# Squared-ReLU attention and a low-rank mixer on one core: block turns held between a cast and its turn, and casts of loads put in another order and at other times

## The chip, the cores and the metric

The kernel runs on one core of a Trainium2 chip. The metric is the device time of one execution in microseconds (us). The time before is the median of three executions, 986.9 us (986.28 to 986.96).

A core has five engines that run their own instruction queues in order: PE (TensorE, matrix products), DVE (VectorE), ACT (ScalarE), POOL (GpSimd) and SP (SyncE), which in this kernel issues every transfer. Tiles in SBUF have 128 partitions; PE writes its sums into PSUM.

## The reference

```python
B, S, D, dqk, R, H = 8, 3136, 256, 64, 32, 1024
# attention unit
scores = (1 / S) * z @ z.transpose(0, 2, 1)          # S x S for each batch, symmetric
attn   = maximum(scores, 0) ** 2
x      = u * (attn @ v)                              # B x S x D
# mixer
h   = x.transpose(0, 2, 1) @ U @ V                   # rank 32 over the sequence
x2  = x + h.transpose(0, 2, 1)
out = x2 + maximum(x2 @ w_ch1, 0) @ w_ch2
```

The inputs and the output are float32. The products are made in bfloat16 and summed in float32.

## The kernel before

**Tiles and items.** The 3136 rows of a batch are 24 tiles of 128 and a tail of 64. Four tiles are a group, so a batch has six groups of 512 rows and a small one of 64 (`NQ` = 6, `NG` = 7). An item is a pair (batch b, group g); the kernel goes through the 56 items in slots, t = 7 b + g. Slot 6 is thus the small item of batch 0, and slot 7 the first of batch 1. A slot of a full group takes some 13 to 19 us, a small one some 2 us for batch 0.

**What one slot does.** For its own item it forms attn @ v (`av_stream`, `av_end`) in a stream of units of one pair of 64-row matmuls each, and multiplies by u (`av_out`, L734). Between the units it places the scores of a later item (`score_burst`; eviction with ReLU L386 or L382, square L362), and the mixer of items seven and more slots back: `t1_all` (L782, the product with U for a whole batch), `u2_unit` (product with V, then x + h on DVE, L855), `ch1_part` (product with w_ch1) and `ch2_stream` (product with w_ch2). The small items have their own routines (`av_small`, L701, whose four partial sums go through ACT L720 and DVE L722, L724; `score_small`; `ch2_small`).

**Blocks and block turns.** A block holds 512 x 512 of attn in bfloat16. There are 20 of them in a list of free blocks. As scores are symmetric, a block (J, g) with J > g is computed once and transposed into a second block for item J by a DMA of SP, the block turn (`issue_turn`, L416; a block on the diagonal has a smaller one, L408). The turn takes its destination from the list of free blocks, and waits until PE has read what stood in it. A block whose score is squared puts its turn on the list `ready_turns`.

**The turn of x + h.** `ch1_part` needs x + h transposed (`u2T`). `u2_unit` adds x and h on DVE; three units before that ends, by the planner's books, `down` gives out the cast of x + h to bfloat16 on ACT or DVE, and two units after the cast's end `turned` gives out the transposing DMA (`x_turn`, L770), again on SP. For group 0 of a batch the cast is on DVE at once, and (b, g) is put on the list `urgent` right there; `turned` clears that list.

**The planner.** The order of the instructions on each queue is worked out while the program is written. `clock` counts in units of one pair of 256-column matmuls; `free_at` books when ACT, DVE and SP are free; `hold(due, f)` keeps a piece of work until the clock has come to its due time; `run_held` gives out what is due, and then block turns, as long as SP's books are free and `urgent` is empty. `cast` takes ACT or DVE, whichever the books have free first (L202, L204). When the matmuls of a block are written out and its turn is still in `ready_turns`, `av_stream` gives it out at once. When a piece of v that they need has no cast yet, it runs the held work until there is one.

**Loads and their casts.** Loads for batch 1 and the weights are given out in slots 0 to 5, each 22 units after the one before it: in slots 1 and 2 two quarters of V each (L1197) and a piece of v, in slot 3 U and two pieces of v, in slots 4 and 5 two pieces of w_ch1 (L1171) or w_ch2 (L1174) and a piece of v (`load_v_piece`, L254). Their casts are collected in `casts_next` and held in the next slot: 45 units after its start (15 units from slot 8 on, 90 units in a small slot), and 12 units more for each further one. `load_part` makes the steps for z and v, `first_loads` those for V, U and the weights.

Of the kernel before, what the change touches and what calls it, by code (L numbers as in the profile page):

```python
# [18 lines left out]
def kernel(  # L19
# [13 lines left out]
    B, S, D = u.shape  # L33
# [21 lines left out]
    NG = len(groups)  # L55
    items = [(b, g) for b in range(B) for g in range(NG)]

    def tiles_of(g):
        g0, gw = groups[g]
        return [(q, g0 // P + q, min(P, gw - q * P)) for q in range((gw + P - 1) // P)]  # L60
# [16 lines left out]
    NQ = NF // GT  # L77
# [18 lines left out]
    clock = [0.0]  # L96
# [4 lines left out]
    urgent = []  # L101
# [9 lines left out]
    def book(eng, ready, cost):  # L111
        free_at[eng] = max(free_at[eng], ready) + cost
        return free_at[eng]
# [5 lines left out]
    def hold(due, f):  # L119
        held.append((due, len(held), f))  # L120
# [25 lines left out]
    def take_ps():  # L146
        k = min(range(NPS), key=lambda i: ps_free[i])
        assert ps_free[k] < float("inf")
        clock[0] = max(clock[0], ps_free[k])
        ps_free[k] = float("inf")  # L150
        for bank in range(2):
            wrote.pop((k, bank), None)
        return k, ps_pool.tile([P, 2, GW], FP32, name=f"ps{k}")
# [23 lines left out]
    def pair(k, ops, n):  # L177

        if any(wrote.get((k, bank), (h,))[0] != h for h, bank, _ in ops):
            post(k)  # L180
        for h, bank, args in ops:
            ins = nc.tensor.matmul(**args)  # L182
            last = wrote.get((k, bank))
            if last and last[0] != h:
                behind(ins, last[2])
            wrote[k, bank] = [h, ins, None]
        pe(n / 256)
# [11 lines left out]
    def cast(out, in_, n):  # L199

        if free_at["act"] <= free_at["dve"]:
            nc.scalar.copy(out=out, in_=in_)  # L202
            return book("act", clock[0], n / 110)
        nc.vector.tensor_copy(out=out, in_=in_)  # L204
        return book("dve", clock[0], n / 130)

    def stage():
        return pool.tile([P, GT * D], FP32, name="stage", bufs=3)
# [13 lines left out]
    def load_z_piece(b, t0, n, raw, tail=True):  # L222
        m = min(n, NF - t0)
        nc.sync.dma_start(
            out=raw[:, : m * dqk].rearrange("p (t d) -> p t d", d=dqk), in_=rows_of(z[b])[:, t0 : t0 + m, :]
        )
        queued(m * dqk / 2)
        if n > m and tail:

            def tails():  # L230
                load_tail(raw, m * dqk, z[b], dqk)
                load_tail(raw, n * dqk, v[b], D)

            if b > 1:
                hold(clock[0] + 75, tails)
            else:
                tails()

    def z_copy(b, t0, n, raw, c, copy):
        copy(out=z_bfs[b][:, t0 : t0 + n, c, :], in_=raw[:, : n * dqk].rearrange("p (t d) -> p t d", d=dqk))  # L240

    def z_tiles(b):
        z_bfs[b] = pool.tile([P, NT, 2, dqk], BF16, name="z_bf", bufs=1)
        zzTs[b] = pool.tile([P, NT, P], BF16, name="zzT")
        v_bfs[b] = pool.tile([P, NT, D], BF16, name="v_bf")

    def v_tail(b, n, raw, copy):
        copy(out=v_bfs[b][:, NF, :], in_=raw[:, n * dqk : n * dqk + D])
        v_cast.add((b, NQ))
# [3 lines left out]
    def load_v_piece(b, k, raw):  # L253
        nc.sync.dma_start(  # L254
            out=raw.rearrange("p (t d) -> p t d", d=D), in_=rows_of(v[b])[:, k * GT : (k + 1) * GT, :]
        )
        queued(GT * D / 2)

    def v_copy(b, k, raw, copy):
        copy(out=v_bfs[b][:, k * GT : (k + 1) * GT, :], in_=raw.rearrange("p (t d) -> p t d", d=D))  # L260
        v_cast.add((b, k))

    def by_cast(n):
        return lambda out, in_: cast(out, in_, n)
# [6 lines left out]
    def load_part(b, g):  # L271
        later = {1: [0], 2: [1], 3: [2, 3], 4: [4], 5: [5]}

        def z_step(t0, n):
            raw = stage()
            load_z_piece(b, t0, n, raw)

            todo = []
            where = spare_next if b == 1 else todo
            copy = nc.gpsimd.tensor_copy if b == 1 else None  # L280
            for c in range(2):
                where.append(
                    lambda t0=t0, n=n, raw=raw, c=c: z_copy(b, t0, n, raw, c, copy or by_cast(n * dqk))
                )
            if n != 4 * GT:
                where.append(lambda n=n, raw=raw: v_tail(b, n, raw, copy or by_cast(D)))
            return todo

        def v_step(k):
            raw = stage()  # L290
            load_v_piece(b, k, raw)
            return [lambda k=k, raw=raw: v_copy(b, k, raw, by_cast(GT * D))]

        steps = []
        if g == 0:
            z_tiles(b)
            steps += [lambda: z_step(0, 4 * GT), lambda: z_step(4 * GT, NT - 4 * GT)]
        for k in {1: [0], 2: [1], 3: [2], 4: [3, 4], 5: [5]}.get(g, []) if b > 1 else later.get(g, []):
            steps.append(lambda k=k: v_step(k))
        return steps  # L300
# [322 lines left out]
    def crossed(way, a, make):  # L623

        ops = []
        for h in range(2):
            bank = h if way == 0 else 1 - h
            ops.append((h, bank, make(slice(h * hp, (h + 1) * hp), a + 2 * bank)))
        return ops
# [178 lines left out]
    def u2_unit(b, g, turn=True):  # L808
        ts = tiles_of(g)
        n, t0, rows = len(ts), ts[0][1], ts[0][2]  # L810
        k, ps = take_ps()
        if n == GT:
            for a in range(2):
                pair(
                    k,
                    crossed(
                        0,
                        a,
                        lambda h, q: dict(
                            out=four(ps)[:, q, :],  # L820
                            lhsT=V4_bf[h, (t0 + q) * P : (t0 + q + 1) * P],
                            rhs=t1s[b][h, :],
                            start=(a == 0),
                            stop=(a == 1),
                        ),
                    ),
                    D,
                )
        else:
            pair(  # L830
                k,
                [
                    (
                        0,
                        0,
                        dict(
                            out=ps[:, 0, :D],
                            lhsT=V4_bf[:hp, t0 * P : (t0 + 1) * P],
                            rhs=t1s[b][:hp, :],
                            start=True,  # L840
                            stop=True,
                        ),
                    )
                ],
                D,
            )
        x = xs[b, g][:rows, :n, :]
        if b == B - 1:
            entry, raw = stage_block()
            o_blocks[b, g] = entry  # L850
            o = raw.rearrange("p (q d) -> p q d", d=D)
        else:
            o = pool.tile([P, GT, D], FP32, name="out_sb", bufs=3)
        done = ps_free[k] = book("dve", clock[0] + 3, 11.2 * n / GT)
        nc.vector.tensor_tensor(out=o[:rows, :n, :], in0=four(ps)[:rows, :n, :], in1=x, op=ALU.add)  # L855
        u2s[b, g] = o
        if not turn:
            return

        def turned():  # L860
            u2Ts[b, g] = u2T_tile()
            x_turn(b, g, u2Ts[b, g])
            urgent.clear()

        def down():
            hold(cast(x, o[:rows, :n, :], n * D) + 2, turned)

        if g == 0:
            urgent.append((b, g))
            nc.vector.tensor_copy(out=x, in_=o[:rows, :n, :])  # L870
            hold(book("dve", done, 6.3) - 6, turned)
        else:
            hold(done - 3, down)
# [316 lines left out]
    def load_V(i0):  # L1190
# [25 lines left out]
    first_loads = {  # L1216
        1: lambda: load_V(0),
        2: lambda: load_V(2),
        3: lambda: [load_U],
        4: lambda: load_w(0),  # L1220
        5: lambda: load_w(1),
    }
# [84 lines left out]
    for b in range(B):  # L1307
        for g in range(NQ):
            t = b * NG + g - 1
# [24 lines left out]
    for t in range(n_items):  # L1334
# [6 lines left out]
        g_now = t % NG  # L1341
        b_next = t // NG + 1
# [6 lines left out]
            xTs[direct] = take_block()[1][:, : GT // 2, :].rearrange("p a (q d c) -> p (a q) d c", d=ND, c=P)  # L1349
            x_turn(*direct, xTs[direct])  # L1350
        for i, f in enumerate(casts_next):
            hold(clock[0] + (90 if g_now == NQ else 15 if t > NG else 45) + 12 * i, f)
        casts_next = []
        spare += spare_next
        spare_next.clear()
        steps = first_loads[t]() if t in first_loads else []
        if b_next < B:
            steps += load_part(b_next, g_now)

        def load(step):  # L1360
            casts_next.extend(step())
# [155 lines left out]
```

## Time and profile before

| what | us |
|---|---|
| median of three executions | 986.9 |
| the profiled execution, its own time | 988.19 |
| its span, first to last instruction | 986.4 |
| PE busy in the span | 974.8 |
| DVE / ACT busy | 627.8 / 483.6 |
| slot 6 and most of slot 7, 95.0 to 105.0: PE, DVE, ACT busy of 10.0 | 10.0, 8.66, 7.84 |
| 105.0 to 115.0: PE, DVE, ACT busy of 10.0 | 8.23, 6.56, 5.86 |
| one batch in the middle (441.6 to 561.4): PE, DVE, ACT busy of 119.8 | 119.8, 77.5, 56.2 |

The view of waits adds up, for an engine and a line, the idle time that ended when another engine or a DMA released it. The chain of waits goes back from the last instruction, at each step to what released it. The timeline lists instructions in order with their start and length; SPq rows are DMAs being issued on SP, and they include the time for which the issue waits in the queue. "u2T<-x_bf" is the turn of x + h, "blk<-blk" a block turn.

The transfers, with the median time from issue to landing:

```profile
stage<-in_v_dram SPq DMA_DIRECT2D x42, 512.0 KB, 6.2
blk<-blk SPq DMA_TRANSPOSE x156, 5.1
blk<-in_moe_w_ch_dram SPq DMA_DIRECT2D x4, 512.0 KB, 4.7
u2T<-x_bf SPq DMA_TRANSPOSE x47, 4.0
```

### The profile page before, as it was taken

The page shows a single profiled execution, that of the slowest core. Times are in us where ns is not written, and L with a number is a line of the kernel's source. Part 1 is how long each engine was busy: PE and PEld are TensorE (multiplying, and loading weights), DVE is VectorE, ACT ScalarE, POOL GpSimd, SP SyncE. Part 2 cuts the span into 40 slices and gives each one's busy share as a digit, 9 for nine tenths or more (in the row PEclk, how much of TensorE's full clock was granted, in tenths as well). Part 3 has the DMA queues.
Part 4 walks back from the last instruction along what each step waited for, and adds up shares of the span by engine and source line. Part 5 has one row for each costly group of instructions (what it writes and reads, how often), then busy time and mean ns, then how long its engine had stood idle before and what let it go on. Part 6 is the DMA issues. An engine that isn't in the chain of part 4 may idle for free.

```text
span 986.4 us, 35362 instructions
## 1 busy us (share of the span) xinstructions
PE 974.8 (99%) x16165; PEld 780.2 (79%) x16165; DVE 627.8 (64%) x809; ACT 483.6 (49%) x562; POOL 16.6 (2%) x25
## 2 busy tenths in 40 slices
PE   9999999999999999999999999999999999999998
PEld 6798788877778778787777877788777887778766
DVE  7877755668556685567755667566775567653363
ACT  7887732456324573345633555334554346431353
POOL 4100000000000000000000000000000000000000
PEclk9999999999999999999999999999999999999999
DMA  9999999979997699897999679997899878954143
GB/s 264 208 252 181 205 205 199 197 155 190 203 192 174 151 196 217 205 151 171 180 224 209 135 178 195 227 184 137 171 214 224 179 136 167 193 121 100 49 113 99
DMA packets 372405, 176.37 MB, mean 179 GB/s; under 512 B 347296, under 2 KB 350624, under 8 KB 372256
## 3 DMA queue, kind: packets, MB, share of 16 engines
q1 hardware_dynamic: 372256, 174.12, 86.9%
q8 instruction: 126, 2.06, 0.9%
q14 instruction: 23, 0.19, 0.1%
HBM read 62.56 MB, written 25.69 MB: 89 GB/s over the span
## 4 chain that ended last, share of the span: by engine, by line
PE 94%; DVE 2%; ACT 2%; DMA 1%; SPq 1%; issue 0%; DVEq 0%; POOL 0%; POOLq 0%
PE ps L182 91%; DVE blk L362 1%; PE ps L701 1%; DMA u2T<-x_bf 1%; ACT blk L386 1%; PE ps L782 1%; PE ps L1080 0%; SPq L416 0%; DVE blk L382 0%; PE ps L1284 0%; ACT blk L946 0%; PE ps L329 0%; SPq L1197 0%; PE ps L327 0%; DVE x_bf L734 0%
## 5 line engine op out<-in xcount | busy, mean ns | idle before, releaser
L182 PEld LDWEIGHTS <-blk 64*128 64x128 bf16 x12288 | 615.6, 94 | 153.6 <-POOLq L172 9.9
L182 PE MATMUL ps<-v_bf,blk 64*128 64x256 bf16 x9216 | 612.1, 269 | 1.9 <-ACT v_bf L202 1.8
L386 ACT ACTIVATE blk<-ps 128x1024 bf16<-128x1024 f32 (+1 forms) x334 | 314.8, 972 | 346.4 <-PE ps L182 341.6
L362 DVE TENSOR_TENSOR blk<-blk 128x1024 bf16<-128x1024 bf16 x351 | 223.1, 660 | 46.8 <-ACT blk L386 46.1
L182 PE MATMUL ps<-u2T,w_bf 64*128 64x512 bf16 (+1 forms) x1792 | 227.8, 349 | 1.6 <-DMA u2T<-x_bf 1.5
L182 PE MATMUL ps<-w_bf,blk 64*128 64x256 bf16 x3072 | 192.4, 269 | 0.2 <-ACT blk L946 0.2
L943 DVE TENSOR_SCALAR blk<-ps 128x1024 bf16<-128x1024 f32 x105 | 128.5, 1224 | 94.5 <-PE ps L182 93.9
L946 ACT ACTIVATE blk<-ps 128x1024 bf16<-128x1024 f32 x87 | 88.3, 1022 | 118.3 <-PE ps L182 118.0
L182 PE MATMUL ps<-zzT 64*128 64x512 bf16 (+2 forms) x902 | 130.8, 328 | 1.3 <-ACT blk L386 0.5
L182 PEld LDWEIGHTS <-w_bf 64*128 64x128 bf16 x1792 | 84.6, 94 | 28.8 <-POOLq L172 5.0
L734 DVE TENSOR_TENSOR x_bf<-ps,u_sb 128x1024 bf16<-128x1024 f32 x48 | 58.6, 1222 | 72.3 <-PE ps L182 72.2
L855 DVE TENSOR_TENSOR out_sb<-ps,x_bf 128x1024 f32<-128x1024 f32 x42 | 51.4, 1223 | 59.5 <-PE ps L182 59.5
L1066 DVE TENSOR_TENSOR out_sb<-ps,out_sb 128x1024 f32<-128x1024 f32 x42 | 51.4, 1224 | 18.7 <-PE ps L182 18.3
L182 PEld LDWEIGHTS <-zzT 64*128 64x128 bf16 x902 | 41.8, 94 | 7.3 <-issue 2.7
L382 DVE TENSOR_SCALAR blk<-ps 128x1024 bf16<-128x1024 f32 (+1 forms) x14 | 16.1, 1147 | 11.0 <-PE ps L182 10.1
L182 PE MATMUL ps<-t_sb,V_bf 64*128 64x256 bf16 x200 | 20.6, 269 | 0.0
L204 DVE CAST v_bf<-stage 128x1024 bf16<-128x1024 f32 (+1 forms) x33 | 20.2, 611 | 0.0
L182 PE MATMUL ps<-v_bf,last_sb 64*128 64x256 bf16 x192 | 18.5, 269 | 0.2 <-POOLq L172 0.2
L202 ACT CAST v_bf<-stage 128x1024 bf16<-128x1024 f32 x15 | 15.6, 1043 | 0.0
L204 DVE CAST x_bf<-out_sb 128x1024 bf16<-128x1024 f32 x21 | 14.5, 688 | 0.3
L202 ACT CAST x_bf<-out_sb 128x1024 bf16<-128x1024 f32 x14 | 14.5, 1037 | 0.0
L362 DVE TENSOR_TENSOR attn_small<-attn_small 128x1600 bf16<-128x1600 bf16 x8 | 7.9, 991 | 9.0 <-ACT attn_small L591 9.0
(80 smaller groups left out, 240.6 us busy)
## 6 DMA issues: line engine op xcount, KB each, us to landing
u_sb<-in_u_dram SPq DMA_DIRECT2D x48, 512.0 KB, 5.2
stage<-in_v_dram SPq DMA_DIRECT2D x42, 512.0 KB, 6.2
out_dram<-out_sb SPq DMA_DIRECT2D x42, 512.0 KB, 3.1
stage<-in_z_dram SPq DMA_DIRECT2D x7, 512.0 KB, 6.1
blk<-in_v_dram SPq DMA_DIRECT2D x5, 512.0 KB, 6.1
out_dram<-blk SPq DMA_DIRECT2D x5, 512.0 KB, 2.6
blk<-blk SPq DMA_TRANSPOSE x156, 5.1
blk<-in_moe_w_ch_dram SPq DMA_DIRECT2D x4, 512.0 KB, 4.7
```

The costliest lines, as they stand in the source:

```text
L182: ins = nc.tensor.matmul(**args)
L202: nc.scalar.copy(out=out, in_=in_)
L204: nc.vector.tensor_copy(out=out, in_=in_)
L362: nc.vector.tensor_tensor(out=a, in0=a, in1=a, op=ALU.mult)
L382: nc.vector.tensor_scalar(out=dst, in0=src, scalar1=scale, scalar2=0.0, op0=ALU.mult, op1=ALU.max)
L386: nc.scalar.activation(out=dst, in_=src, func=AF.Relu, scale=scale)
L701: nc.tensor.matmul(out=ps[c * hp : c * hp + rows, h, :D], lhsT=smalls[b][h * hp : (h + 1) * hp, place_of(jt), :], rhs=v_bfs[b][h * hp : (h ...
L734: nc.vector.tensor_tensor(out=xs[b, g][:rows, :n, :], in0=four(box["ps"])[:rows, :n, :], in1=u_sbs[b, g][:rows, :n, :], op=ALU.mult,)
L855: nc.vector.tensor_tensor(out=o[:rows, :n, :], in0=four(ps)[:rows, :n, :], in1=x, op=ALU.add)
L943: nc.vector.tensor_single_scalar(out=r, in_=ps[:, :, :gw], scalar=0.0, op=ALU.max)
L946: nc.scalar.activation(out=r, in_=ps[:, :, :gw], func=AF.Relu)
L1066: nc.vector.tensor_tensor(out=o, in0=acc, in1=o, op=ALU.add)
```

## The change

It has three parts. `down` puts (b, g) on `urgent` when it gives out the cast of x + h, for every group and not only for group 0, so that `run_held` gives out no block turn until `turned` has given out the turn of x + h and cleared the list. The casts held over into slot 6 are due 15, 27 and 39 units after its start and no longer 90, 102 and 114 (in the small slots of later batches it stays 90; slot 7 has none to hold). In slots 1 to 5 the steps for v come ahead of those for V, U and the weights, and so do their casts a slot later.

```diff
@@ -863,6 +863,7 @@
             urgent.clear()
 
         def down():
+            urgent.append((b, g))
             hold(cast(x, o[:rows, :n, :], n * D) + 2, turned)
 
         if g == 0:
@@ -1349,13 +1350,12 @@
             xTs[direct] = take_block()[1][:, : GT // 2, :].rearrange("p a (q d c) -> p (a q) d c", d=ND, c=P)
             x_turn(*direct, xTs[direct])
         for i, f in enumerate(casts_next):
-            hold(clock[0] + (90 if g_now == NQ else 15 if t > NG else 45) + 12 * i, f)
+            hold(clock[0] + (90 if g_now == NQ and b_next > 1 else 15 if t >= NQ else 45) + 12 * i, f)
         casts_next = []
         spare += spare_next
         spare_next.clear()
-        steps = first_loads[t]() if t in first_loads else []
-        if b_next < B:
-            steps += load_part(b_next, g_now)
+        steps = load_part(b_next, g_now) if b_next < B else []
+        steps += first_loads[t]() if t in first_loads else []
 
         def load(step):
             casts_next.extend(step())
```

## The prediction

> **What bounds the kernel now.** I read the head of the page first.
>
> ```profile
> span 986.4 us, 35362 instructions
> PE 974.8 (99%) x16165; PEld 780.2 (79%) x16165; DVE 627.8 (64%) x809; ACT 483.6 (49%) x562; POOL 16.6 (2%) x25
> ```
>
> TensorE (PE) is busy for 974.8 of 986.4 us and its row of granted clock is full in every slice. The change takes no matmul away, so it can only give back idle time of PE, or make more of it. The view of waits, for PE alone, says where the idle time is:
>
> ```profile
> PE ps L182 <- ACT v_bf L202: 1.8, 1, 1.8
> PE ps L182 <- DMA u2T<-x_bf: 1.5, 2, 0.9
> PE ps L1284 <- POOL ident masks.py:199: 1.4, 1, 1.4
> ```
>
> The columns are the total, the times and the longest. The third line is the start, which the change does not reach. The first two are what it aims at. The other rows are 0.7 us and less each. The timeline shows the places: PE stops 1.77 us before 108.61 us, 0.54 us before 132.52 and 0.92 us before 255.12. Between 255.12 us and the last 47 us PE has no wait at all, and a period of one batch is 119.83 us there. Whatever comes earlier at 255 us therefore comes earlier at the end.
>
> The chain that ended last, in order of time, gives the cause of the first two:
>
> ```profile
> 104.75 1.02 ACT blk L386
> 105.77 0.93 ACT w_bf L202
> 106.70 0.93 ACT blk L386
> 107.62 0.94 ACT v_bf L202
> 108.57 0.04 issue
> 108.61 15.64 PE ps L182 x240
> ...
> 125.32 0.70 DVE blk L362
> 126.03 0.90 SPq L416
> ...
> 127.02 5.45 DMA u2T<-x_bf
> 132.47 0.05 issue
> 132.52 66.78 PE ps L182 x1084
> ```
>
> At 104.75 ScalarE (ACT) has no gap: evictions and casts alternate, and the cast of batch 1's last piece of v is the very last, at 108.55; the matmuls on it start at 108.61. At 125 the turn of x + h (L770) stands in SP's queue behind a block turn (L416) that waited for a square ending at 126.01. Its own input, the cast on ACT at 121.71, was done at 122.75. It lands at 132.47, after PE wants it. SP's timeline shows the third place:
>
> ```profile
> 242.98 7.43 SPq L416 DMA_TRANSPOSE blk<-blk  x2
> 250.50 1.53 SPq L770 DMA_TRANSPOSE u2T<-x_bf  x1
> 252.14 5.32 SPq L416 DMA_TRANSPOSE blk<-blk  x2
> ```
>
> The first of the two block turns waits 5.0 us for PE to give up its destination block and is over at 248.13; the second runs from there to 250.41; the cast has been ready since 245.04.
>
> **Part 1, the casts.** In slot 6 (the small item of batch 0, from 93.8 us) three casts lie ready: two of w_ch2 and v piece 5. Before, they are due 90, 102 and 114 planner units after the slot's start, v last. A unit is one pair of 256 columns; 32 matmuls in 1.91 us, less 0.27 for the last one's drain, make 0.107 us. So 9.6 to 12.2 us: slot 6 is only about 18 units long, and the casts fall deep in slot 7, which is where the trace has them (104.20 on DVE, 105.65 and 107.50 on ACT). Afterwards v is due at 15 units, the weights at 27 and 39: 1.6, 2.9 and 4.2 us after 93.8, about 95.4, 96.7 and 98.0 us, the first given out behind the four sums of the small item. Landed by then? The three loads were issued by 87.34 and take 4.7 to 6.2 us: by 93.6. Yes. PE wants v at 106.84, so this stall goes whole: **-1.77 us**. Nothing slides into its place: the block before it was squared by 106.69, and ACT loses two casts (2.10 us) and DVE one (0.68) out of 102.85 to 108.55.
>
> What the casts meet where they go: behind the small copy at 95.89 ACT has two evictions (1.94 us), then the copy for t1 (98.49), then DVE's two steps, and PE takes t1 at 100.25 with L796 over at 99.56. A v cast of 1.05 us on ACT ahead of the evictions moves t1 to 100.6: 0.35 us late at most. The planner books that copy too and issues the unit when a PSUM slot is free, so between 0 and 0.4 I take **+0.2**. The weights cost 0.68 (DVE) or 1.05 (ACT) each; ACT's idle 0.40 us before 99.25 and 1.17 before 102.85 take them. Without those gaps they would push evictions by about a microsecond, which stalls PE only if the other PSUM slots are full too.
>
> **What is late next.** The turn of group 0's x + h is issued at 103.33 and lands 7.2 us later, at 110.53; PE uses it at 112.31. With PE 1.77 us ahead that is 110.54: no slack is left. Its input comes from DVE, which from 97.67 to 103.07 has 0.2 us idle, so one weight cast ahead costs up to 0.5. Bounds: 0 if the landing also comes earlier, 1.77 if it slips as far as the cast gained; I take **+0.3**, nearer to the DVE cast's row. The Trainium skill (DMA: Bandwidth & Descriptors, section Queues, rings and completion order) says that each DMA engine takes descriptors in the order of its ring; by that, the landing is set by the two u loads issued at 102.18 ahead of it, and an earlier PE does not move it. The trace agrees so far that this landing took 7.2 us while others took as little as 2.3; by the rule the sum stays, and the first rival below is likelier.
>
> **Part 2, the turns held back.** Between the cast being given out and its turn, no block turn is given out any more. At 124.68 us, when the first block turn is off SP, the next instruction is the turn of x + h: 2.3 us sooner than 127.02. With the old 5.45 us it lands at 130.1; PE wants it at 131.98, or 130.2 if PE is 1.77 us ahead and SP is not: the 0.54 goes, **-0.54**, though by 0.1 us in that worst case. At 248.13 likewise instead of 250.50; landing 4.57 later, 252.7 against a want at 254.20: **-0.92**. In later batches the same pattern has no stall (issued 368.94, landed 3.3 later at 372.2, used 374.96), so nothing is won there. What waits instead: one block turn per slot is issued about 20 units (2.1 us) later, and behind it on SP the store of the output, the load of u and that of v. The blocks so moved are mostly those of group 5, wanted two slots (some 37 us) later; a turn takes 5.1 us to land. If the matmuls on a block are written out while its turn is still held, the planner gives the turn out at once. Cost 0, covered by that distance; if the cover were gone it would be up to 2.1 us per slot.
>
> **Part 3, order of loads in slots 1 to 5.** v goes ahead of V, U and the weights: no instruction more or less. The V loads (eight small ones on SP) move 22 units, 2.4 us, later; their use is at 100 us. Casts of v and V change places at about 47 to 55 us, where DVE is busy 9.64 and ACT 9.88 of 10 us and PE still has no wait. The nearest rows of what could come are the stalls of 0.53 and 0.48 us before 39.77 and 45.32: between -0.5 and +0.5. I take 0, as the engines' work there is the same.
>
> **The sum.** -1.77 - 0.54 - 0.92 + 0.2 + 0.3 = -2.73. The profiled execution took 988.19 us (span 986.4 and 1.8 around it): 985.46. It stands 1.3 above the median of 986.9, so on the median **984.2 us**, 0.28% faster. What can be told from no change is about 0.2%, or 2 us: below 984.9 counts as faster, above 988.9 as slower.
>
> **Rivals.**
> First, *the stall moves to group 0's turn*: its landing at 110.53 or later takes all of the cast's 1.77, and only part 2 remains: 986.9 - 1.46 = 985.4. For it: the slack worked out above is 0.01 us. Against: it needs the landing to slip by the whole amount. 0.22.
> Second, *the books are reshuffled and nothing is won*: the planner's choices of engine in slots 1 to 8 move, and stalls of about 0.5 us as before 39.77 and 45.32 appear four to six times: 986.9. For: ACT and DVE are full from 45 to 55. Against: PE has no wait between 45.3 and 106.8 in spite of it. 0.08.
> Third, the other side, *held turns come late in every batch*: a block turn kept back by 2.1 us makes the queue behind it (u, v, output, next turns) late, so that batches 2 to 7 each get a stall like the longest seen for a turn, 0.92: six of them are 5.5, 984.2 + 5.5 = 989.7. It decides when a turn lands less than 2.1 us ahead of its use. For: SP waited 196 us in all for PE at block turns, so the queue is not free. Against: two slots of distance. 0.08.
> That the change does not do what it says, because the block turns were given out ahead of the cast, I rule out for the two places: followed through the code, the planner's clock (an order, no time) has the cast at unit 1060, the block turn at 1079 and the turn of x + h at 1080, and one batch later 2174, 2174 (behind the cast, in the same pass) and 2194.
>
> **Chances.** Forecast 0.62 (from 983.7, nothing of the 3.23 lost, to 985.0, with 0.4 and half of the 1.77 lost; beyond that it is the first rival), rivals 0.22, 0.08, 0.08. Faster takes the forecast, less a little at its edge, and a small part of the first rival: 0.63. Same: 0.28. Slower: 0.09. The range is 983.3 (all three stalls gone, nothing lost, and 0.4 from part 3) to 987.0, which holds the first two rivals and leaves the third out.
>
> **What would show it.** In the changed kernel PE's waits lose the line for v_bf; the casts stand at 95 to 100 us; each L770 after a cast has at most one L416 between them on SP; the two u2T waits are gone, or one new u2T wait stands near 110 us (first rival). L796 ends later than 99.6. Batches 3 to 6 keep 119.83 us each. Wrong would be a stall that repeats from batch to batch, or new PE waits on evictions between 95 and 105 us.

## The result and the profile after

The changed kernel takes 985.11 us, the median of 13 executions (983.88 to 985.75). The kernel before, run beside it, takes 987.32 (13 executions, 985.72 to 988.95). The ratio is 0.9977, with a 95% interval of 0.9970 to 0.9984: faster by 0.16 to 0.30%. The profiled executions have spans of 984.0 and 986.4 us.

The page of the changed kernel, its head (engine, busy time, share of the span, instructions):

```profile
span 984.0 us, 35373 instructions
PE 974.5 (99%) x16165; PEld 778.2 (79%) x16165; DVE 630.0 (64%) x811; ACT 484.3 (49%) x560; POOL 16.5 (2%) x25
```

PE does the same work; what went is idle time. The view of PE's waits in the changed kernel (total, times, longest):

```profile
PE ps L182 <- ACT blk L386: 1.5, 2, 0.9
...
PE ps L182 <- DVE x_bf L734: 0.5, 1, 0.5
...
PE ps L182 <- DMA u2T<-x_bf: 0.2, 1, 0.2
```

The line for v_bf is gone, and of the 1.5 us for u2T 0.2 are left. But the wait for ACT's evictions (L386), 0.5 us before, is 1.5 now. The timeline of PE has the two new places (start, length, and in brackets the idle time ahead and who ended it):

```profile
55.02 0.39 PE L182 MATMUL ps<-zzT 64*128 64x512 bf16 x2 [0.94 <-ACT blk L386]
...
111.82 0.60 PE L182 MATMUL ps<-u2T,w_bf 64*128 64x512 bf16 x4 [0.18 <-DMA u2T<-x_bf]
```

SP's queue around the turn that came too late at 127.02 us before:

```profile
117.70 3.75 SPq L416 DMA_TRANSPOSE blk<-blk  x1
122.28 2.05 SPq L770 DMA_TRANSPOSE u2T<-x_bf  x1
124.43 4.83 SPq L416 DMA_TRANSPOSE blk<-blk  x2
```

The turn of x + h (L770) now goes out behind one block turn, and two come after it.

**Accounting by stage.** One matmul (L578) is issued once per batch; in the kernel before the first four stand at 76.29, 88.92, 199.12 and 321.61 us. PE's wait for DVE near 45 us is in every trace. This wait and the first, third and fourth L578 cut the span into stages that can be set side by side; the first 45 us are left out, for a reason given at the end. Each row is one profiled execution. In us:

| kernel | 45 us to 1st L578 | 1st to 3rd | 3rd to 4th | 4th to the end | sum |
|---|---|---|---|---|---|
| before | 30.97 | 122.83 | 122.49 | 664.80 | 941.09 |
| changed | 32.07 | 120.41 | 121.41 | 664.79 | 938.67 |
| changed_again | 32.08 | 120.05 | 121.41 | 664.79 | 938.33 |
| turns_only | 30.97 | 122.00 | 121.40 | 664.80 | 939.16 |
| due_only | 30.97 | 121.53 | 122.04 | 664.79 | 939.33 |
| order_only | 32.09 | 120.67 | 121.81 | 664.78 | 939.35 |
| order_slot5 | 30.96 | 120.05 | 121.41 | 664.80 | 937.22 |
| order5_due90 | 30.96 | 121.24 | 121.50 | 664.80 | 938.49 |
| order5_due90_again | 30.97 | 120.18 | 121.41 | 664.80 | 937.36 |
| V_on_dve | 30.96 | 120.06 | 121.40 | 664.80 | 937.22 |
| v15_w90 | 30.97 | 120.19 | 121.41 | 665.28 | 937.85 |
| order5_due90_ulate | 30.96 | 120.06 | 121.49 | 664.79 | 937.30 |
| order_slot5_ulate | 30.97 | 120.05 | 121.41 | 664.79 | 937.21 |

The changed kernel wins 2.42 us in the second stage and 1.08 in the third, loses 1.10 in the first, and nothing happens in the 665 us after that: 2.42 us in sum, against 2.4 between the spans. How far one execution differs from the next on the same program can be seen in two pairs of rows: the second stage by 0.36 us (changed and changed_again) and by 1.06 (order5_due90 and its second execution), the others by 0.09 at most.

### The profile page after: what moved, and what is told of

It reads as the page before. It is cut to its first block, busy times and chain, and to the rows that moved or that the text cites. A ratio compares the mean times of both kernels' runs of the same rounds, so it can differ in the third digit from the quotient of the medians.

```text
span 984.0 us, 35373 instructions
## 1 busy us (share of the span) xinstructions
PE 974.5 (99%) x16165; PEld 778.2 (79%) x16165; DVE 630.0 (64%) x811; ACT 484.3 (49%) x560; POOL 16.5 (2%) x25
## 4 chain that ended last, share of the span: by engine, by line
PE 94%; DVE 2%; ACT 2%; DMA 1%; SPq 0%; POOL 0%; issue 0%; DVEq 0%; POOLq 0%
PE ps L182 91%; DVE blk L362 1%; PE ps L701 1%; ACT blk L386 1%; PE ps L782 1%; DMA u2T<-x_bf 1%; DMA blk<-in_moe_V_dram 0%; PE ps L1081 0%; DVE blk L382 0%; PE ps L1285 0%; ACT blk L947 0%; PE ps L329 0%; POOL v_bf L1246 0%; PE ps L327 0%; SPq L1198 0%
## 5 line engine op out<-in xcount | busy, mean ns | idle before, releaser
L386 ACT ACTIVATE blk<-ps 128x1024 bf16<-128x1024 f32 (+1 forms) x331 | 312.1, 971 | 343.8 <-PE ps L182 341.7
L734 DVE TENSOR_TENSOR x_bf<-ps,u_sb 128x1024 bf16<-128x1024 f32 x48 | 58.7, 1222 | 72.8 <-PE ps L182 72.8
L382 DVE TENSOR_SCALAR blk<-ps 128x1024 bf16<-128x1024 f32 (+1 forms) x17 | 19.6, 1159 | 7.1 <-PE ps L182 7.1
L202 ACT CAST v_bf<-stage 128x1024 bf16<-128x1024 f32 x18 | 18.7, 1042 | 0.0
L204 DVE CAST v_bf<-stage 128x1024 bf16<-128x1024 f32 (+1 forms) x30 | 18.1, 603 | 0.0
```

The lines of the kernel that those rows point to most:

```text
L382: nc.vector.tensor_scalar(out=dst, in0=src, scalar1=scale, scalar2=0.0, op0=ALU.mult, op1=ALU.max)
L386: nc.scalar.activation(out=dst, in_=src, func=AF.Relu, scale=scale)
L734: nc.vector.tensor_tensor(out=xs[b, g][:rows, :n, :], in0=four(box["ps"])[:rows, :n, :], in1=u_sbs[b, g][:rows, :n, :], op=ALU.mult,)
```

## The experiments

All runs were compared with the kernel before on the same chip; each ratio has its 95% interval. The stages are those of the table above.

**turns_only**: the kernel before with the line in `down` alone.

```diff
         def down():
+            urgent.append((b, g))
```

> Only the line in down: block turns held back, casts and load order as before. Theory A (three separate stalls, each part of the change has its own): PE's two u2T waits (0.54 and 0.92 us) are gone, the v_bf wait of 1.77 us stays; span 986.4 - 1.46 = 984.9, ratio about 0.9985. Rival B (the u2T waits went because casts left ACT earlier and moved PE against SP, not because turns are held): u2T waits stay near 1.5 us in total, span 986.4.

Measured: 985.49 us, ratio 0.9990 (0.9980 to 1.0000). Both u2T waits are gone and the v_bf wait of 1.77 stays. The turn is issued at 124.58 us. Rival B falls. The gain by stages is 0.83 and 1.09, 1.93 in sum, not the 1.46 of PE's waits.

**due_only**: only the expression of the due time changed.

> Only the due times of the casts in slot 6 (15, 27, 39 units), in the old order: weights first, v last. Theory A: the v_bf wait is gone (v cast some 2.6 us later than in the changed kernel, still before 106.8), the 0.94 us wait for ACT near 55 us is absent since the order of loads is the old one, the u2T waits near 132 and 255 us stay or grow: span 986.4 - 1.8, plus up to 1 us for a late turn of group 0 near 110 us: 984.6 to 985.6. Rival B: the u2T waits of 0.54 and 0.92 are gone here too, span about 983.5.

Measured: 985.38 us, ratio 0.9996 (0.9986 to 1.0005). The v_bf wait is gone. Three u2T waits stand in the trace, the new one first and the last, of 0.45 us, at 251.91:

```profile
109.68 0.60 PE L182 MATMUL ps<-u2T,w_bf 64*128 64x512 bf16 x4 [0.59 <-DMA u2T<-x_bf]
...
129.88 0.61 PE L182 MATMUL ps<-u2T,w_bf 64*128 64x512 bf16 x4 [0.54 <-DMA u2T<-x_bf]
```

So here, without held turns, the stall at 130 us stays and rival B falls, and the one at 110 us is what the first rival of the prediction spoke of: the second stage wins 1.30. The span of 983.2, below what theory A expected and near rival B's 983.5, is no gain of the change: its first 45 us were 1.45 us shorter.

**order_only**: only v ahead of the other loads, all due times as before.

> Only the order: v ahead of V, U and weights in slots 1 to 5, casts in slot 6 still due at 90, 102, 114, so v at 90. Theory A: the 0.94 us wait near 55 us is here (both V casts on ACT), the u2T waits stay, and the v cast at 90 units (about 104 us) ends before PE wants it, so the 1.77 is gone without the early due time: span 986.4 - 1.77 + 0.94 = 985.6. Rival C (the early due time is what removes the v_bf wait): a v_bf wait of 0.5 us or more remains, span 986.5 or more.

Measured: 985.07 us, ratio 0.9988 (0.9979 to 0.9998). The v_bf wait is gone although v's cast is due at 90 units (it runs on DVE at 103.70), and the wait of 0.94 us is there, at 53.42. Rival C falls: v being the first of the three casts is enough. The first stage loses 1.12 us. The u2T waits did not stay as theory A expected: there is none near 130 us, 0.24 us at 251.78, and a new one of 0.45 at 110.48. The turn of slot 8, issued at 123.30 behind two block turns as before, landed in 3.8 us and not in 5.5. So that stall can go without held turns too, and what these are worth beside v first is not shown by itself: no run has the whole change without them.

**order_slot5**: the whole change, but in slots 1 to 4 the loads keep the old order.

```diff
         steps = load_part(b_next, g_now) if b_next < B else []
-        steps += first_loads[t]() if t in first_loads else []
+        first = first_loads[t]() if t in first_loads else []
+        steps = steps + first if t == NQ - 1 else first + steps
```

> The whole change, but v goes first only in slot 5; slots 1 to 4 load in the old order. Theory A: the 0.94 us wait near 55 us is gone, as one V cast is on DVE again (1.11 us instead of 2.08 on ACT); the turn of group 0 is still issued late (weights' casts and an eviction on DVE ahead of it), so a u2T wait of 0.2 to 1.1 us stands near 110 us: span 984.0 - 0.9 + up to 0.9: 983.1 to 984.0. Rival D (the 0.94 comes from elsewhere, such as SP's V loads or the early v cast): it stays, span 984.0.

Measured: 984.29 us, ratio 0.9977 (0.9968 to 0.9987). The wait near 55 us is gone and no u2T wait is left; 3.87 us less than before from 45 us to the end. Rival D falls. The turn of group 0 is still issued late (104.67), but landed in 4.6 us, so the u2T wait that theory A expected did not come.

**V_on_dve**: the whole change, with the four large casts of V always on DVE.

```diff
-                cast(
...
-                    2 * n * NF,
-                )
+                nc.vector.tensor_copy(
...
+                )
+                book("dve", clock[0], 2 * n * NF / 130)
```

> The whole change, with the four big casts of V always on DVE. Theory A (the 0.94 us wait near 55 us comes from two casts of V at 2.08 us on ACT in the place of one there and one of 1.11 us on DVE): that wait is gone or under 0.3, and from PE's wait near 45 us to the milestone at 77 us it takes 31.0 us and not 32.1. Rival F (two V casts close together hurt on any engine): a wait of 0.5 us or more for DVE or for an eviction between 47 and 58 us, 31.5 or more.

Measured: 982.93 us, ratio 0.9969 (0.9956 to 0.9982), five executions. The wait is gone, the first stage is 30.96. ACT's timeline at this place, first the kernel before, then the changed one:

```profile
46.84 2.11 ACT L202 CAST V_bf<-blk 128x768 bf16<-128x768 f32 x1
48.83 7.68 ACT L386 ACTIVATE blk<-ps 128x1024 bf16<-128x1024 f32 x8
```

```profile
46.83 1.06 ACT L202 CAST v_bf<-stage 128x1024 bf16<-128x1024 f32 x1
48.13 1.02 ACT L386 ACTIVATE blk<-ps 128x1024 bf16<-128x1024 f32 x1 [0.24 <-PE ps L182]
49.05 2.08 ACT L202 CAST V_bf<-blk 128x768 bf16<-128x768 f32 x1
51.03 1.03 ACT L386 ACTIVATE blk<-ps 128x1024 bf16<-128x1024 f32 x1
51.95 2.09 ACT L202 CAST V_bf<-blk 128x768 bf16<-128x768 f32 x1
53.93 2.86 ACT L386 ACTIVATE blk<-ps 128x1024 bf16<-128x1024 f32 x3
```

Before, ACT had one cast of V and then eight evictions with no gap, and DVE the other cast (1.11 us) and v's. With v first, v and both V casts go to ACT, 2.08 and 2.09 us of them, and the evictions between them come late: the one at 53.93 is what PE waited for at 55.02. In V_on_dve the two casts stand on DVE:

```profile
48.18 1.11 DVE L1202 CAST V_bf<-blk 128x768 bf16<-128x768 f32 x1
...
49.81 1.10 DVE L1202 CAST V_bf<-blk 128x768 bf16<-128x768 f32 x1
```

The cause of the loss in the first stage is shown: the engine that these casts fall to. Rival F falls.

**order5_due90**, run twice: turns held, v first in slot 5, and the three casts due at 90, 102 and 114 again.

> Turns held back, v first in slot 5 only, and the casts of slot 6 due at 90, 102, 114 as before. From PE's wait for DVE near 45 us to the end the kernel before takes 941.1 us. Theory A' (the order of the three casts matters, not their due time: v at 90 units ends near 104 us, before 106.8, and at 90 the casts stand behind the turn of group 0): no v_bf wait, turn of group 0 issued near 103.3, no u2T wait, 937.2 from there to the end, as with the due times of the change. Rival E (the early due time is needed): a v_bf wait or a wait for an eviction of 0.3 us or more near 107 us, 937.6 or more.

> order5_due90 a second time, to see how far the landing of group 0's turn varies from execution to execution on the same program. Theory H: 7 to 9 us after its issue again, about 9 us after the two u loads were issued, u2T wait of 0.5 to 1.3 us. Rival I says the same; a landing under 6 us would say that this wait is chance.

Measured: 984.33 us, ratio 0.9977 (0.9966 to 0.9988), and 983.09 in the second, a single execution. Both agree that no v_bf wait is left and that the turn of group 0 is issued early, 58.0 us after PE's wait near 45 as before. But in the first profile it took 8.2 us to land and PE waited 1.0 us for it; in the second 7.1 us, and no wait of PE is shown (0.2 us of the weight loads). The early due time is not needed against the v_bf wait; whether group 0's turn then comes late is a matter of how long it takes to land, which differs from execution to execution. So neither theory A' nor rival E holds whole.

**v15_w90**: as order_slot5, with only v early and the weights' casts at 102 and 114.

> Turns held back, v first in slot 5 only, v's cast due at 15 units and the two casts of weights at 102 and 114. Theory A (weights' casts ahead of t1 and of x + h are what made group 0's turn late, 105.91 against 103.33): that turn is issued near 103.3 to 103.9, and there is no u2T wait; 937.2 from PE's wait near 45 us to the end. Rival G (v's cast on ACT alone, by pushing evictions to DVE, makes the turn late): issued at 104.5 or later.

Measured: 983.86 us, ratio 0.9968 (0.9955 to 0.9981). No u2T wait. Counted from PE's wait near 45 us, the turn of group 0 is issued after 58.7 us, between 58.0 (before, order5_due90) and 59.5 (order_slot5): v's cast at 15 units makes it 0.7 late and the weights' casts another 0.8. Both theories have a part. The 0.5 us more in the last stage belong to one batch of this execution, behind a wait at 346.77 us that no engine ended; the edit changes nothing behind slot 7, and the cause of this wait is open.

**changed_again**: the changed kernel itself.

> The changed kernel once more on this chip, to stand beside the three others. All theories: from PE's wait near 45 us to the end 938.7 us, as in its first profile, with the waits of 0.94 us near 55 us and about 0.2 near 111.8; only the first 45 us may differ by up to 1.5 us, as two kernels with the same start have shown (the wait for DVE at 45.3 and at 43.8 us).

Measured: 984.01 us, ratio 0.9976 (0.9967 to 0.9985). The wait of 0.94 us repeats; the u2T wait at 111.8 does not, as the turn landed in 4.2 us after 5.9 in the first profile.

**order5_due90_ulate and order_slot5_ulate**: the load of u of slot 7 is given out behind the turn of group 0.

```diff
-            hold(clock[0] + 60, lambda t=t: load_u(*items[t + 1]))
+            hold(clock[0] + (105 if t == NG else 60), lambda t=t: load_u(*items[t + 1]))
```

> As order5_due90 (turns held, v first in slot 5, casts at 90), but the load of u given out in slot 7 is due 105 and no longer 60 units after that slot's start, so it is issued behind the turn of group 0's x + h and not ahead of it. Theory H (this turn lands when the bytes ahead of it in SP's ring have moved, whatever its own issue time): it lands 2 us or more sooner after its issue than the 8.2 us of order5_due90, the u2T wait of 1.0 us near 110 us is gone, and from PE's wait near 45 us to the end it takes 937.2 us. Rival I (the transposing DMA itself is slow there, through the block turn beside it): 7 us or more from issue to landing, u2T wait of 0.5 us or more, 938 or more.

> As order_slot5 (the whole change with v first in slot 5 only), with the same load of u behind the turn. All waits that this study has followed are gone already in order_slot5, so theory H and rival I both give 937.2 us from PE's wait near 45 us to the end, as there; under theory H the turn of group 0 has a microsecond or more to spare, landing within 5 us of its issue.

Measured: 984.04 us, ratio 0.9966 (0.9955 to 0.9977), and 983.60 us, ratio 0.9966 (0.9953 to 0.9978). SP's timeline of order5_due90 and then of order5_due90_ulate:

```profile
100.83 1.05 SPq L306 DMA_DIRECT2D u_sb<-in_u_dram  x2
101.97 1.24 SPq L770 DMA_TRANSPOSE u2T<-x_bf  x1
```

```profile
101.90 0.58 SPq L306 DMA_DIRECT2D u_sb<-in_u_dram  x1
102.82 1.23 SPq L770 DMA_TRANSPOSE u2T<-x_bf  x1
```

With one load of u ahead of it the turn lands in 5.7 us, with two in 8.2 and 7.1; in order_slot5_ulate in 3.4, in order_slot5 in 4.6. The u2T wait is gone, as it was in order5_due90_again without this edit. Theory H agrees with this, the margin of its "2 us or more" only against the first of the two executions. The other traces fit it as well: where two u loads were issued in the 2.1 us ahead of this turn, it landed in 6.8 to 8.2 us (five executions), with one in the 1.8 us ahead in 4.6 to 6.3 (four), and with none in the 3 us ahead in 3.4 to 5.9 (four). The last two ranges overlap, and the same program gave 8.2 and 7.1, so this is a tendency and no fixed price. Both kernels take less time than the kernel before; against the two executions of the changed one the stages say 1.0 to 1.5 us less, 1.1 of them the first stage's loss, and the intervals of the ratios overlap.

## Why the prediction was right, and where its sum was off

The forecast was 984.2 us, 2.73 less than before. The direction and the size came out: 2.42 by the stages, 0.23% by the ratio. But the terms were not what was written.

**The stalls were worth more.** The prediction took 1.77, 0.54 and 0.92 from PE's waits, 3.23 in all. The weight loads of the kernel before have another idle time at the same three places (PEld, the idle time in brackets):

```profile
108.61 0.77 PEld L182 LDWEIGHTS <-blk 64*128 64x128 bf16 x15 [1.95 <-issue]
```

```profile
132.51 0.11 PEld L182 LDWEIGHTS <-w_bf 64*128 64x128 bf16 x4 [0.82 <-DMA u2T<-x_bf]
```

```profile
255.12 0.11 PEld L182 LDWEIGHTS <-w_bf 64*128 64x128 bf16 x4 [1.20 <-DMA u2T<-x_bf]
```

1.95, 0.82 and 1.20, and the stages gave back 1.95, 0.83 and 1.08: 122.83 to 122.00 with the turns alone, 122.00 to 120.05 with the cast as well, 122.49 to 121.41. The sum is 3.86. PE's waits were 0.16 to 0.29 us short each. The likely reason, which no run here tests, is that the last matmul before a stall counts as busy until its modelled end. The Trainium skill (Perfetto Trace Analysis, its part on the Tensor Engine instruction) says that the end of a matmul in the profile is computed and not observed; this case's traces agree, with 3.23 of idle time for 3.86 of gain. The two stalls of the changed kernel say the same: PE's waits are 0.94 and 0.18 there, the gaps of the weight loads 1.24 and 0.46, and they cost 1.10 and 0.36. Over all five places the gaps come to 5.67 us, PE's waits to 4.35 and the cost to 5.32.

**Part 3 was the term that failed.** The prediction had the order of loads at 0, "as the engines' work there is the same", between -0.5 and +0.5. It cost 1.10 us, outside those bounds. The work was not the same: a cast of V takes 1.11 us on DVE and 2.1 on ACT, and the order decides which engine it falls to. Of the four large casts of V, two are on ACT in the kernel before and three in the changed one. The planner does not see the difference: its books have such a cast at 1536/110 = 14.0 units on ACT and 1536/130 = 11.8 on DVE, at 0.107 us a unit 1.5 and 1.3 us. The bounds of the prediction were taken from stalls of another cause, not from the two rows of the same cast on two engines, which the trace of before has. The warning was there (DVE at 9.64 and ACT at 9.88 of 10 us); it was read as cover because PE had no wait.

**Group 0's turn.** The prediction gave it no slack and +0.3 us, with DVE late by up to 0.5. The chain of the changed kernel shows how late it was (start, length, what):

```profile
97.56 0.95 ACT v_bf L202
98.53 1.94 ACT blk L386 x2
...
101.60 1.29 DVE blk L362 x2
102.89 1.14 DVE blk L382
104.03 1.14 DVE out_sb L855
105.19 0.69 DVE x_bf L871
105.91 5.86 DMA u2T<-x_bf
111.82 86.16 PE ps L182 x1396
```

Behind the casts an eviction moved from ACT to DVE (L382, 1.14 us on the chain), ahead of x + h. The turn is issued 2.58 us later than before, 1.1 of them the stall near 55 us; the other 1.5 are three times the 0.5. It still cost only 0.36 us of the second stage here and nothing in changed_again, because the landing took 5.9 and 4.2 us and not 7.2. The prediction also weighed that the two u loads ahead set the landing, whenever the turn is issued. That came out in part: the u loads were issued at 102.37 and before at 102.18, the turn 2.58 us later, and it landed at 111.77 and before at 110.53, 1.24 later. The first rival took place, without its full price, and that its price was small owes something to how long this landing happened to take.

**Point by point.** The casts at 95 to 100 us: the trace has v at 97.46 on ACT and the weights at 99.70 and 100.77, after a stall of 1.1 us ahead of them. The v_bf stall went as forecast, but the early due time was not needed for it: due_only has it with v still last, order_only and order5_due90 with v first at 90 units, and no v_bf wait is left in any of them. The +0.2 for t1 is not seen: L796 ends at 101.56, beyond the stall 0.9 us later than before and not 0.35 at most, but there is no wait of PE, and order_slot5 has the whole 1.95. The turn of x + h in slot 8, expected at 124.68 us, was issued at 124.58 in turns_only. It landed 3.8 us later, and its stall went with room to spare; the one at 255 us too, where the turn was issued at 245.15 and not only at 248.13. The third rival, turns late in every batch, did not occur: the stage from the fourth L578 to the end is 664.78 to 664.80 us in every kernel but v15_w90. The second rival had its mechanism, the choice of engine, but at one place and not at four to six.

The sum by its own terms, with what they measured: -1.95 - 0.83 - 1.08 + 1.10 (order of loads) + 0.36 (group 0's turn) = -2.40. It was forecast as -3.23 + 0.5 = -2.73: two errors, 0.63 too little gain and 0.96 too little loss, mostly cancelled. That the total came within a few tenths of a microsecond is luck to that extent. That the terms add up to the measured 2.42 is no test of them, as they are differences between rows of the one table; the parts also overlap, as order_only shows.

## What to carry to other kernels

Where PE is busy 99% of the time, look for the few stalls by place and ask for each who was queued ahead of the late piece: one line that holds transposes back won 1.93 us by itself, and casting v earlier, or ahead of two other casts, up to 1.95. In these traces the gap in the weight loads was nearer to the price of a stall than PE's idle time. Before an order is changed "at no cost" in a stretch where two engines are full, look whether the moved pieces take the same time on both, and whether the planner's books say so; a planner that balances by booked time can send them to the other engine. And a turn that has no slack is better not put behind loads that nobody needs yet.

## What the runs showed that was not expected

**Two starts.** The same instructions take 1.1 to 1.7 us more or less for the first 45 us, from profile to profile: PE's wait for DVE stands at 45.32 us in the kernel before and at 43.87 in due_only, at 45.31 in the changed kernel and at 43.88 in changed_again. PE's timeline shows where it begins, in the kernel before and then in due_only:

```profile
6.42 1.22 PE L327 MATMUL ps<-ident 128*128 128x128 bf16 x10 [0.69 <-ACT blk L376]
```

```profile
6.34 0.72 PE L327 MATMUL ps<-ident 128*128 128x128 bf16 x10 [0.69 <-ACT blk L376]
```

Ten matmuls take 1.22 or 0.72 us, though the profile's row of granted clock is full from the first slice. The next eight take 1.06 or 0.61, the four after them 1.04 or 0.61. In all thirteen profiles this goes with the start: in the six where the ten take 1.22 or 1.23 us, PE's wait for DVE stands at 45.0 to 45.4, in the seven where they take 0.72 at 43.7 to 44.0. The Trainium skill (TensorE: Matmul & The Clock Gate, Part 1) says that PE runs at half rate until a window of activity that runs freely, not from the kernel's start, has been busy. The two starts agree with that, but no run here set the window's phase. The times of the changed kernel fall into two heaps (983.88 to 984.14 and 985.11 to 985.75). The two profiled executions fit: 985.75 has the long start, 984.02 of changed_again the short one; of the others the start is not known. The heaps stand apart by over half of what the change is worth, and the median of 985.11 is the lowest time of the upper one, so medians of about ten executions move with the mix. The stages leave the start out.

**Casts.** Rounding float32 to bfloat16 takes ACT 1.05 us for 128 x 1024 in a row and 2.08 to 2.11 for 128 x 768 read with a step of 24 elements (V, L1202); DVE takes 0.69 and 1.11. No run here tests whether the step is the reason.
